# Another order of issue for the steps of a DeltaNet and MLP-mixer kernel

## The chip, the cores and the metric

The kernel runs on one core of a Trainium2 chip, as one program with one launch. The core has a matrix engine (TensorE, PE in the profile, with its weight loads shown apart as PEld), three engines for elementwise work (VectorE, DVE; ScalarE, ACT; GpSimd, POOL) and SyncE (SP), which here issues the DMA transfers. Each of them works through its own instructions strictly in the order in which the program issued them, and waits at an instruction until what it needs is there.

The metric is the time on the device in microseconds, as the median of several runs.

## The reference

Four batches of 768 tokens go through eight heads of a DeltaNet attention (head size 48), and its output, 384 wide, through an MLP mixer that mixes first over the tokens and then over the channels. All values are float32.

```python
k_n = k / (np.linalg.norm(k, axis=-1, keepdims=True) + 1e-06)   # q, k, v: (4, 8, 768, 48)
state = np.zeros((B, H, D, D)); y = np.zeros_like(q)
for t in range(S):
    kt, vt, bt = k_n[:, :, t], v[:, :, t], beta[:, :, t, None]
    y[:, :, t] = np.einsum('bhd,bhde->bhe', q[:, :, t], state)
    v_old = np.einsum('bhde,bhd->bhe', state, kt)
    state = state + bt[:, :, :, None] * np.einsum('bhd,bhe->bhde', kt, vt - v_old)

x = y.transpose(0, 2, 1, 3).reshape(B, S, H * D)                # (4, 768, 384)
xt = x.transpose(0, 2, 1)
h = np.maximum(xt @ w_tok1, 0.0) @ w_tok2                       # 768 -> 256 -> 768
u = x + h.transpose(0, 2, 1)
out = u + np.maximum(u @ w_ch1, 0.0) @ w_ch2                    # 384 -> 1536 -> 384
```

## The kernel before

The attention is computed in chunks of 64 tokens: inside a chunk a triangular matrix made from the keys is inverted, and from chunk to chunk a state of 48 x 48 for each head is carried on. The kernel divides the work into 24 *units* of 128 tokens of one batch (all eight heads, two chunks). Units 0 to 5 are batch 0, 6 to 11 batch 1, and 12 to 23 batches 2 and 3 in turn. The inversion takes units in rounds: round 0 is units 0 to 3, round 1 units 4 and 5, round 2 units 6 to 9, and so on to round 6. The recurrence is a chain for each batch, 12 chunks long, in which each link needs the state that the one before left.

Everything is written as *jobs*. A job is a Python generator that issues a few instructions and then yields, so that each `next` of it is one *step*. A step puts its instructions at the end of the queues of the engines that carry them. The text `order` (from line 1775) lists the steps of the whole kernel, 2,610 of them; `p0*5` stands for five steps of job `p0` in a row. The loop behind the text issues them in that order, and nothing else sets the order of the instructions on an engine:

```python
    for word in order.split():
        name, _, n = word.partition("*")
        for _ in range(int(n or 1)):
            next(jobs[name])
```

So a step that stands early in the text may hold up, on an in-order engine, a step behind it that has nothing to do with it, if its own input is late. The jobs, with the lines that appear in the profile:

- `k0` to `k23` load a unit's keys and queries (DMAs issued by SP, lines 391, 420, 444, into `kst` and `pads`); for the first four units ACT copies the keys (line 435). `v0` to `v23` load the values in four pieces on SP, and POOL scales them by beta (lines 457 to 484).
- `b` loads beta for all batches (line 252), turns it with small products (48 in the profile) into `p_b` (line 257), and ACT copies the result to `beta_st` (line 261). The scaling of keys and values needs it.
- `p0` to `p23` prepare a unit: ACT squares the keys (line 539), DVE sums them (542), ACT takes the square root (547, 548), DVE the reciprocal and its product with beta, `cs` (551, 552), PE transposes keys and queries (562, 582), ACT copies them out of PSUM (566, 587), and POOL makes the mask `mb` from `cs` (574).
- `c0` to `c23` and `d0` to `d11` are a unit's products of keys with keys and queries, `p_g` (PE, line 511, 32 for a unit of batches 0 and 1), with DVE's mask multiplication after them (517).
- `t0` to `t23` cut these into the small pieces that the inversion works on (lines 674 to 686; from unit 6 on through DRAM, `n_dram`). `i0` to `i6` are the rounds of inversion, nearly all DVE (lines 731 to 760). `f0` to `f23`, `h0` to `h11` and `j0` to `j23` put the inverted pieces together again (697 to 711; 777 to 795, among them ACT's copies on line 795; 813 to 892).
- `r0` to `r11` are the recurrences of batch 0, chunk by chunk, `r12` to `r23` those of batch 1 (lines 920 to 972; ACT copies the chunk's new values out of `p_w` on line 950), and `r24` to `r35` those of batches 2 and 3 together (1009 to 1091).
- `m0` and `m1` are the mixer for batches 0 and 1 (products on lines 1593, 1608, 1668 and 1689). Batches 2 and 3 go through `T2`, `T3`, `W`, `S`, `s`, `l` and the groups `A`, `F`, `B` (from line 1098 to 1583), in which products are saved by sums and differences of blocks.
- `w0` to `w33` bring in the mixer's weights, one block of 128 rows each. The weights come as 64-bit words; SP loads a block into one of three buffers `d64` that are used in turn (line 280), two ACT steps (286, 287), one on DVE (289) and one on POOL (293) make rounded float32 of it, and POOL's step frees the buffer. `q0` to `q5` put part of the last weights aside in DRAM.
- `x`, `z` and `Y` compute nothing that is used. `x` is one product of zeros, 128 columns wide (line 235), `z` the same with four times the columns, and `Y` a group of four small products of zeros (line 245; the profile shows each float32 product as two, so eight). They go to a PSUM buffer `p_warm` that nothing else uses in this part of the kernel, and wait for no data.

## Time and profile before

| | us |
|---|---|
| Three runs: lowest, median, highest | 620.05, 625.72, 627.02 |
| The profiled execution, first to last instruction (span) | 619.7 |

The span leaves out only what lies around the first and the last instruction; the profiled execution stands beside the fastest of the three runs.

Engine shares of the whole span hide a good deal here, since it has stages of different kinds: an opening in which the first units are loaded and prepared, the inversion of the first four units, the chain of recurrences with the preparation of later units, from the end of batch 0's on with its mixer beside the rest, and last the mixer of batches 2 and 3. The page's view by slices (40 of 15.5 us each, busy share in tenths) shows where each engine works:

```profile
DVE  5987875986889855697566996866888898685874
ACT  8758796448521344223551215415352331414200
POOL 2348264225311122003020120010000000000000
DMA  9667567667653254454445443135102012020001
```

ACT and DMA are busy at the front, DVE throughout, and POOL nearly only in the first third. The costliest groups of the page are those of the mixer: its columns are line, engine, operation, tiles and forms, count, then busy time and mean ns of one, then idle time just before it and what ended most of that.

```profile
L1668 PE MATMUL p_c<-u_t,wc 128*128 128x256 f32 x432 | 101.6, 386 | 0.5 <-issue 0.5
L1689 PE MATMUL p_o<-wc,r 128*128 128x192 f32 x360 | 64.6, 331 | 0.7 <-DVE xb L1628 0.7
```

The clock that was granted to PE, the row `PEclk`, stands in tenths of full speed for each slice.

### The profile page before, as it was taken

The numbers are of one execution on the slowest core, as the hardware profiler recorded it, in microseconds if no ns is written. First come the engines' busy times: TensorE is split into PE (matmuls) and PEld (weight loads), VectorE is DVE, ScalarE is ACT, GpSimd is POOL, SyncE is SP. The second block draws the span as 40 slices with busy tenths as digits, with TensorE's granted clock in tenths as the row PEclk, the third lists the DMA queues.
The fourth block names the chain that finished last, engine by engine and source line by source line (L and its number), as shares of the span: only waits on it lengthen the run. The fifth ranks groups of instructions, "written<-read, shape, count | busy, mean of one in ns | idle before, by whom it ended". The sixth has DMA issues, their size and how long they took to land.

```text
span 619.7 us, 20909 instructions
## 1 busy us (share of the span) xinstructions
PE 590.3 (95%) x8733; PEld 515.9 (83%) x8733; DVE 469.1 (76%) x1160; ACT 256.9 (41%) x682; POOL 109.9 (18%) x150
## 2 busy tenths in 40 slices
...
DVE  5987875986889855697566996866888898685874
ACT  8758796448521344223551215415352331414200
POOL 2348264225311122003020120010000000000000
PEclk9878797999999999999999999999999999999999
DMA  9667567667653254454445443135102012020001
GB/s 219 136 135 169 138 142 185 129 155 179 126 114 72 67 116 83 95 113 99 92 87 126 83 95 83 32 66 140 32 2 39 1 21 47 12 52 13 14 26 51
DMA packets 154605, 55.52 MB, mean 90 GB/s; under 512 B 129648, under 2 KB 148976, under 8 KB 154512
## 3 DMA queue, kind: packets, MB, share of 16 engines
...
q14 instruction: 25, 0.20, 0.1%
...
## 4 chain that ended last, share of the span: by engine, by line
PE 74%; DVE 9%; DMA 4%; ACT 4%; issue 2%; SPq 1%; POOL 1%; DVEq 0%; POOLq 0%; ACTq 0%
PE p_c L1668 13%; PE p_r L1498 13%; PE p_o L1689 10%; PE p_a L1570 7%; PE p_b L1570 6%; PE p_g L511 3%; DMA d<-in_moe_w_ch_dram 3%; PE p_h L1608 3%; DVE sub L739 2%; PE p L1593 2%; DVE x L744 2%; PE p_k L920 2%; PE p L1223 1%; PE p_h L1238 1%; PE p_y L1034 1%
## 5 line engine op out<-in xcount | busy, mean ns | idle before, releaser
L1668 PE MATMUL p_c<-u_t,wc 128*128 128x256 f32 x432 | 101.6, 386 | 0.5 <-issue 0.5
L1668 PEld LDWEIGHTS p_c<-u_t,wc 128*128 128x128 f32 x432 | 79.6, 190 | 11.9 <-issue 1.1
L1689 PE MATMUL p_o<-wc,r 128*128 128x192 f32 x360 | 64.6, 331 | 0.7 <-DVE xb L1628 0.7
L739 DVE TENSOR_TENSOR sub<-x 128x84 f32<-128x84 f32 (+24 forms) x178 | 58.4, 328 | 7.4 <-DMA x<-n_dram 2.8
L744 DVE TENSOR_TENSOR x<-x,sub 128x84 f32<-128x84 f32 (+24 forms) x178 | 58.2, 327 | 6.1
L1689 PEld LDWEIGHTS p_o<-wc,r 128*128 128x128 f32 x360 | 58.4, 190 | 2.3 <-DVE xb L1628 1.3
L1677 ACT ACTIVATE r<-p_c 128x512 f32<-128x512 f32 x36 | 21.4, 596 | 51.2 <-PE p_c L1668 46.1
L511 PE MATMUL p_g<-kq 48*64 48x128 f32 (+1 forms) x704 | 34.9, 283 | 4.0 <-ACT kq L587 3.3
L517 DVE TENSOR_TENSOR gm<-p_g,mb 128x512 f32<-128x512 f32 x44 | 28.9, 683 | 8.1 <-PE p_g L511 7.5
L484 POOL TENSOR_TENSOR v_st<-v_st,nrm 128x384 f32<-128x384 f32 x12 | 10.3, 856 | 131.9 <-DMA v_st<-in_v_dram 104.4
L574 POOL TENSOR_TENSOR mb<-mask_c,cs 128x512 f32<-128x512 f32 x20 | 21.2, 1062 | 67.8 <-DVE cs L552 36.9
L511 PEld LDWEIGHTS p_g<-kq 48*64 48x64 f32 (+1 forms) x704 | 26.5, 137 | 7.6 <-ACT kq L587 4.3
L293 POOL TENSOR_TENSOR wc<-w_f,d 128x384 uint32<-128x384 uint32 x24 | 24.6, 1029 | 42.8 <-ACT d L287 14.1
L1511 DVE TENSOR_TENSOR kq<-kq,p_r 128x384 f32<-128x384 f32 x40 | 21.0, 551 | 10.7 <-PE p_r L1498 8.8
L1498 PE MATMUL p_r<-t_d,wc 128*128 128x192 f32 x160 | 28.8, 326 | 0.0
L1511 DVE TENSOR_TENSOR gm<-gm,p_r 128x384 f32<-128x384 f32 x40 | 21.1, 551 | 8.1 <-PE p_r L1498 5.8
L400 DVE STREAM_TRANSPOSE kq<-pads 128x512 f32<-128x512 f32 x24 | 25.5, 1108 | 2.0 <-PE p_w L1038 1.6
L1498 PEld LDWEIGHTS p_r<-t_d,wc 128*128 128x128 f32 x160 | 26.5, 190 | 0.0
L1689 PE MATMUL p_o<-wc,s 128*128 128x192 f32 x144 | 25.7, 330 | 0.6 <-DVE xb L1628 0.6
L1498 PE MATMUL p_r<-pads,wc 128*128 128x192 f32 x128 | 25.4, 326 | 0.0
L1628 DVE TENSOR_TENSOR xb<-xb,p_o 128x192 f32<-128x192 f32 x42 | 14.6, 348 | 13.0 <-PE p_o L1689 12.6
L1689 PEld LDWEIGHTS p_o<-wc,s 128*128 128x128 f32 x144 | 23.3, 190 | 1.2 <-DVE xb L1628 0.9
...
## 6 DMA issues: line engine op xcount, KB each, us to landing
...
```

The costliest lines, as they stand in the source:

```text
L293: nc.gpsimd.tensor_tensor(out=dst.bitcast(U32), in0=f, in1=lo, op=ALU.add)
L400: nc.vector.transpose(kq_of[p // 2][:, i, :, p % 2].rearrange("f p (s g) -> f p g s", g=G), rows_of[i].rearrange("s p (g d) -> s p g d", g ...
L511: nc.tensor.matmul(p_g[PAR[i ^ cc ^ swap(u)], p], kqt[f, p, cc, 0], kqt[f, p, cc])
L517: nc.vector.tensor_tensor(out=blocks(gm_of(u))[:, :, cc, D:GW].rearrange("s p (two n) -> s p two n", two=2), in0=p_g, in1=made[u][:, :, cc ...
L739: nc.vector.tensor_tensor(out=tmp, in0=y[:, :, 0:s, s : s + 1].to_broadcast([n, k, s, w]), in1=y[:, :, s : s + 1, s + 1 : m].to_broadcast( ...
L744: nc.vector.tensor_tensor(out=y[:, :, 0:s, s + 1 : m], in0=y[:, :, 0:s, s + 1 : m], in1=tmp, op=ALU.add,)
L1498: nc.tensor.matmul(p[:, i], pieces[q // width][:, at : at + 128], f[f"u{n}"], start=first and i == 0, stop=True, skip_group_check=True,)
L1511: nc.vector.tensor_tensor(out=o, in0=o, in1=p, op=op_of(sign))
L1570: nc.tensor.matmul(p, a[:, i], w[:, i // 2, i % 2], start=first and i == 0, stop=True, skip_group_check=True,)
L1668: nc.tensor.matmul(p_c[:, k], piece_of(wc1, cb, f * 128)[:, f * 128 : (f + 1) * 128], u_t[:, cb], start=(cb == 0), stop=(cb == NCB - 1),)
L1677: nc.scalar.activation(r2[:, m], p_c, ACTF.Relu)
L1689: nc.tensor.matmul(p, a[:, m], wc2[:, m, j], start=(start and i == 0), stop=(i == NM - 1), skip_group_check=True,)
```

## The change

Only the text `order` is replaced. Every job is run through as before, each job's own steps keep their order, and the counts of `x` (8), `z` (10) and `Y` (6) stay the same; so the same 2,610 steps are issued, and each engine carries the same instructions in another order. The first nine words, from `w10` to the second `k1*3`, are the same.

In the opening, `b` now stands ahead of `k0`, where its last steps stood behind `k0` and the first of `p0`. The loads `k2`, `k4`, `k5`, `v0`, `v1` and `w6` move forward, `w18`, `w13`, `w17`, `k7` and `k8` back. In the recurrences the preparation of units 8 to 11 and the loads of weights (`w22`, `w24`, `w26`, `w4`, `w19`, `w7`, `w32`) are placed anew. The number of steps issued between a weight's load and its step on ACT, before and after:

| | w22 | w4 | w19 | w32 | w7 | w13 | w18 | w12 | w17 |
|---|---|---|---|---|---|---|---|---|---|
| before | 1 | 1 | 40 | 3 | 2 | 32 | 68 | 83 | 1 |
| after | 8 | 13 | 40 | 1 | 3 | 1 | 2 | 1 | 1 |

The place of a step in the text, counted from the first step: `r8` begins at 613 before and 605 after, `r9` at 643 and 649, `r11` at 749 in both, `m0` at 676 and 684. The six `Y` stood at 106, 231, 234, 748, 864 and 885 and stand at 37, 225, 227, 639, 640 and 641; the `z` stood at 5, 8, 16, 20, 23, 47, 213, 218, 219 and 256 and stand at 5, 8, 16, 22, 23, 158, 159, 200, 201 and 206; the later `x` moved from 123, 161, 166 and 212 to 132, 133, 152 and 157.

The diff, cut to the part from the first step to a little past `r11`; the rest of the text is permuted in the same manner:

```diff
@@ -1773,76 +1773,90 @@
     jobs["y"] = jobs["Y"] = warm_tiles()
     order = """
-    w10 x*4 z w10*2 z w1*4 k1*3 z k1*3 z b p1 z p1 k0*6 p0*2 b*2 p1 w2 p0*5 p1*2
-    w10 p0*2 z w3 w2 c0*3 p0 w3*2 d0*2 w3 c0 p1 c0 d0*3 k2*3 v1 p1*2 w18 k2*2 p1*2
-    c1*2 d1 k2 p2*2 c1 t0 d1 c1*2 d1*3 t0 p2*8 c2*2 w2 d2 c2*3 Y d2 w2 k3*6 p3
-    d2*2 p3 d2 t1*3 x p3*7 c3 k4*5 k7 w13 w18*2 d3*2 v1*2 v0*2 c3*3 v0 c3 d3*3 t0
-    p4*2 t2*3 x t3*2 p4*2 x t3 i0*2 w13 p4*2 w18 w17*2 i0 k4 i0*9 p4 i0*2 p4*2 c4
-    k8 c4*3 w13*2 w6*2 k5*2 v0 k6 k5*2 i0*2 d4*2 k5 x z d4*3 c4 z*2 p5*2 k5 t4 p5
-    h0 h1 h0 w8*2 h1 Y i0 f0 Y p4 f1 h2*2 p5*3 f0*2 w6 h0*5 k6*5 p6 z f2*2 k8*3 p5
-    w6 p5 p3 p5 j0*3 f1*2 h1*5 j0*2 w8*2 w17 f2 h2*3 v0 t4*2 w17 r0*5 p6 h2*2 c5*2
-    v1 w11*2 j1 p5 k7*2 c5 k7 c5 r0 c5 r0*2 w14*2 v1 w11*2 k7*2 p7 d5*5 r1*5 w14*2
-    p6*2 t5 j1 t5*2 r1*2 j1 j2 p7 h3*2 r1*3 p6*3 i1*2 r2*5 k8*2 f3*2 w9 k9*3 j1*2
-    v2*2 i1*3 j2*2 r2*2 f3 i1*2 p6*3 w16 v2 w16*3 r2*2 h3 r2 i1 d6 r3*5 i1*2 w9*3
-    v2 d6 h3 v2 w0 h3*2 r3 h3 d6*2 w0 d6 j3 c6*5 r3*4 w0 j2 w0 p8*2 j2 r4 p8 r4*4
-    k9*3 j3*2 r4*2 i1*2 w24 i1*2 p7*7 r4 c7 r4 r5*5 k10 p9 k10 p9 c7 r4 c7*3 i1
-    w5*2 p7 r5*2 w24*3 r5*3 j3*2 i1 r6*4 w26 v3*5 p9 k11 r6 d7*5 w26*3 p8*3 t6*2
-    r6*2 w5*2 p8*4 v4*2 t6 i1 r6*3 h5*2 h4*2 k10*2 f4*3 c8*2 k10 p10 w28*2 c8*2 r7
-    c8 r7*3 d8*4 p9 d8 w28 h4*5 p9 t6 r7*2 j4 w28 p9*3 r7*2 p9 w7 d9 w7 v4*2 f5*2
-    w27*2 w7*2 d9*4 c9*2 f5 c9*3 t7*2 t8 r7*2 t7*2 j4*2 v4 p10*2 h5 r8*3 w29 t8*3
-    w29 w27*2 r8*2 w29*2 q3 w29 j4*2 r8 w22*4 t9*3 r8*3 p9 r9 p10 r9*3 t9 v5 h5*3
-    j5 i2 r9 w4*2 r8 h5 i2*5 w4 i2 w19*2 k10 w32 p10*2 w32 v7 k12 m0*2 k11 k12 q0
-    v5*3 p10*2 r9*2 j5*2 k11*3 i2*2 r9 w4 i2 j5 i2*3 p10 v5 r9*2 d10*3 r10 v7*2 j5
-    i2*2 r10*4 w12 i2 k12 i2*2 m0 w32 k11 k12 w32 r10*2 m0 p11 k12*4 w19 p11 r10
-    c10 r10 c10 r10 w33 d10*2 q2 Y r11*4 v7 r11*3 w19 c10 q1 w30 c10 r11 k12*2
-    i2*3 r11 v6*4 i2*5 m0*3 i2*5 q5 i2 m0 p11*4 c10 p11 m0 p11*2 m0*2 k12*2 w12
...
+    w10 x*4 z w10*2 z w1*4 k1*3 z k1*3 p1*2 z*2 b*3 k0*6 k2 p0*2 v1 Y p1 v1 p1*3
+    k2 p0*3 w2 p0*5 c0*2 w10 w2*2 d0*2 k2 c0*2 d0*2 c0 d0 w3 k2 k3 w3 k2 k3 k2 w3
+    p1*3 d1 p1 w6 w3 v0 d1 w2 p2 d1 c1 d1 c1 p2 d1 t0 k3 c1 k3 c1*2 k4 p2*3 v0
+    p2*5 t0 c2*2 k3 k5 k3 d2*3 c2 p3*2 w6*2 c2 d2*2 c2 p3*6 x*2 p3 d3*2 c3 d3*2
+    k4*5 t0 d3 t1 p4 c3*3 x c3 w18 w6 w18 x z*2 p4 t2 t1 t2 t1 t2 t3*3 w8 i0 k5
+    p4 k5*2 w8 k5 i0 p5 i0*2 p4 i0 k5 p4 k6 p4 w8 w0 i0 k7 i0 p4 k6*3 p4 v1*2 w0
+    z*2 w18 p4 i0 w8 z c4*2 i0*2 c4 i0*2 d4 c4 w13*2 w18 i0*2 c4 d4 i0*2 Y d4 Y
+    v1 d4*2 k6*2 i0 h1 w0 v0*2 w17*2 h0 h1 t4 f1*2 f0 f1 f0*2 h0 w13*2 p3 w17 h2
+    f2 h2 p5 w11 p5 w0 h0 f2 p4 h0*2 f2 h0*2 p5*2 k7 p5*2 k8 p5 j0 t4 v0 j0 p5 j0
+    h1 w17 h1*3 j1 h1 j0*2 d5*5 c5 p6*2 r0 w11 r0*2 c5*3 k7 w27 c5 r0 k7 r0 p6 h2
+    k7 h2 r0*2 h2*3 r0 h3 k7 t4 t5 p6 r1*4 k8*5 w11*2 r1 h3 j1 j2 t5*2 f3*3 r1*2
+    j1 i1 p6*3 w16 p7 r1 p6 p5 r1*2 v2 p6 w5 p6 j1 r2 j1 w27 r2*2 k9 r2 j2 r2 w27
+    i1*2 d6 r2*2 w27 p7 w16*2 j2 d6*3 r2 p7 w16 r2 r3*2 d6 r3 r2 r3 k10 r3 v2*2
+    p7 p8 i1 c6*5 h3*3 i1 k9 h3 r3*2 j2 h3 j2 k10*2 j3 p7 i1*2 w5*2 v2 w14 r3
+    p7*2 r3 k9 i1 j3 r4*2 p8 r3 w28 v2 w14 r4*2 k9 r4 v3 k9 p7 r4 i1*4 p7 c7*4
+    w14 j3 r4 w5 k11 c7 r4 p7 i1 k9 r4 d7*3 w9 i1 w28*2 i1 r5*2 w9 w14 t6 w9 v3
+    r4 p9 r5 w28 r5*2 d7*2 j3*2 r5*2 w22 i1 w9 p8*4 r5 w22 h4 k11 h4 r5*2 r6 k11
+    p8*3 i1 v3*2 r6*3 v3 r6 h5 v4 h5 r6*2 c8*2 p9 w22 p9 c8 w22 w24 c8*2 f4 d8
+    r6*2 d8*3 p8 r6 r7 d8 r7*4 v4 w24 v4 t7 v4*2 p9*2 w24 w26 t7 f4 p9 t7*2 r7*2
+    p9*3 k10*2 w26 p10 t6*2 t8 r7 t8*2 r7 t8 c9*4 f4 c9 k11 t6 w19 d9*5 w24 r8*3
+    f5 h4 f5 r8 f5 t9*4 h4 w26 h4*3 r8 h5 k11 h5*3 j4*2 j5 h5 j4 q0 p10 j4 r7 j4
+    w19 Y*3 r8*3 w19 r8 p11*2 r9*4 j5 p10*2 r9 w26 k10 i2 r8 i2*2 j5 w4 q3 r9
+    i2*4 p10 r9*3 i2 j5 w4*2 r9 j5 p10*2 w19 m0 i2*5 p10 r10*3 p10 c10 d10 k12
+    w32*2 d10 v5*2 w7 w32 i2 w7 d10*2 i2*2 r10 v5 m0 v5 m0 v5 r10 k11 p9 c10 r10
+    i2*2 d10 w4 c10 k12 p11 q1 i2 k12*2 p11 r10 v7 i2 r10 w29 w32 w12*2 r10*2 q2
+    v7 p10 p11 c10 r11*3 i2 k12*2 r11 p11 w7 m0 i2 r11*2 i2 c10 k12 i2 w29*2 q5
+    k12*4 w7 i2*2 p11 w12 w29 i2*4 k12 v7 w30 i2 v6 r11 p11 r11 v6*2 m0 v6 r11
...
     """
     for word in order.split():
         name, _, n = word.partition("*")
```

104 lines of the change are left out of this document (57 added, 47 removed).

## The prediction

> **What bounds the kernel now.** I read the page first (span, engines, granted clock), then the busy times by stage, then the opening and two later stretches engine by engine, and the chain of waits last.
>
> ```profile
> span 619.7 us, 20909 instructions
> PE 590.3 (95%) x8733; PEld 515.9 (83%) x8733; DVE 469.1 (76%) x1160; ACT 256.9 (41%) x682; POOL 109.9 (18%) x150
> PEclk9878797999999999999999999999999999999999
> ```
>
> PE is busy 95% of the span, but the granted clock dips, and only in the first seven slices of 15.5 us. So the next view is the busy time of each engine by stage; its columns are PE, PEld, DVE, ACT, POOL, then granted clock, DMA share and GB/s. I cut at the start of the first inversion (26.7), its end (43.7), recurrence 0 (52.0), recurrence 8 (96.7) and recurrence 11 (121.1).
>
> ```profile
> 0.00:26.70 26.70, 20.14 (x246) 14.70 (x246) 18.14 (x54) 22.22 (x58) 7.96 (x22) 1.00 0.75 171
> 26.70:43.70 17.00, 11.66 (x129) 7.79 (x130) 15.22 (x39) 6.87 (x17) 6.40 (x6) 0.70 0.79 171
> 43.70:52.00 8.30, 7.04 (x205) 5.68 (x201) 7.23 (x13) 7.90 (x23) 6.44 (x8) 1.00 0.45 90
> 52.00:96.70 44.70, 41.22 (x1228) 36.47 (x1227) 35.39 (x89) 38.02 (x103) 25.25 (x32) 0.89 0.68 155
> 96.70:121.10 24.40, 19.95 (x402) 14.41 (x397) 18.18 (x53) 12.66 (x35) 8.06 (x11) 0.79 0.68 162
> 121.10:619.70 498.60, 490.25 (x6549) 436.84 (x6545) 374.98 (x915) 169.21 (x450) 55.81 (x73) 1.00 0.33 73
> ```
>
> The reader is to see two regimes. After 121.1 us PE works 490.25 of 498.60 us at full clock: another order of the same products can gain at most the 8.35 us left idle there. Before it PE idles 21 us and loses clock, and the limit changes: ACT in the opening (22.22 of 26.70), DVE during the first inversion (15.22 of 17.00), ACT from there to recurrence 8 (7.90 of 8.30, then 38.02 of 44.70), and nothing saturated from 96.7 to 121.1, where waits set the pace. So the change is decided before recurrence 11.
>
> **The change part by part.** Every job keeps its number of steps, x, z and Y too: no work is added or removed, only each engine's queue is reordered. Each part is priced as the shift of a milestone. ACT carries most of them, so its rows come first, in order of time.
>
> ```profile
> 6.97 0.52 ACT L539 ACTIVATE ksq<-kst 128x384 f32<-128x384 f32 x1
> 7.74 1.43 ACT L435 COPY kst<-pads 64x192 f32<-64x192 f32 x4 [0.25 <-DMA pads<-in_k_dram]
> 9.21 0.52 ACT L539 ACTIVATE ksq<-kst 128x384 f32<-128x384 f32 x1
> 9.64 0.48 ACT L261 COPY beta_st<-p_b 128x192 f32<-128x192 f32 x1
> 11.27 0.59 ACT L587 COPY wc<-p_t 128x512 f32<-128x512 f32 x1
> ...
> 38.55 0.72 ACT L754 ACTIVATE r<-r,odd 128x512 f32<-128x512 f32 x1 [4.89 <-DVE r L753]
> 52.77 0.32 ACT L950 COPY rw_t<-p_w 128x192 f32<-128x192 f32 x1
> ...
> 90.56 1.08 ACT L795 COPY gm<-p_x 16x128 f32<-16x128 f32 x4
> 97.13 0.30 ACT L548 ACTIVATE ksum<-nrm,eps 128x8 f32<-128x8 f32 x1
> 97.34 0.54 ACT L286 ACTIVATE d<-d 128x384 f32<-128x384 f32 x1
> 97.78 0.54 ACT L287 ACTIVATE d<-d 128x384 uint32<-128x384 uint32 x1
> 101.02 0.55 ACT L286 ACTIVATE d<-d 128x384 f32<-128x384 f32 x1 [1.93 <-DMA d<-in_moe_w_ch_dram]
> 106.94 0.44 ACT L286 ACTIVATE d<-d 128x256 f32<-128x256 f32 x1 [3.88 <-DMA d<-in_moe_w_tok_dram]
> 111.67 0.56 ACT L286 ACTIVATE d<-d 128x384 f32<-128x384 f32 x1 [1.42 <-DMA d<-in_moe_w_ch_dram]
> ```
>
> ```profile
> 7.83 1.57 PE L257 MATMUL p_b<-pick,b_rows 32*64 32x16 f32 x48
> 11.91 1.37 PE L511 MATMUL p_g<-wc 64*64 64x128 f32 x32 [0.18 <-ACT wc L587]
> 30.31 1.09 PE L582 MATMUL p_t<-ident,pads 128*128 128x128 f32 x4 [5.38 <-DMA pads<-in_q_dram]
> ```
>
> *The opening, up to the first inversion.* Job b (beta's load, 48 products into p_b, ACT's copy of them) now stands ahead of k0's copies. The same nine x and z products stand ahead of p_b in both orders, so p_b still ends near 9.4. Before, ACT did k0's copies and square (1.43 + 0.52) while p_b ran; now it waits from 7.49 (6.97 + 0.52) to 9.4 and does them afterwards. That is 2.0 us, on the engine that bounds the opening. Ahead of the inversion's first step ACT also gains w6's pair (1.1, as at 97.34 and 97.78) and loses p4's square root and square (0.5): +0.6. Sum: the inversion starts 2.6 us later, at 29.3. Bounds: +1.4 (w6's pair falls into a pause of ACT, and 0.6 of the wait is made up) to +3.8 (1.2 more, were POOL's w6, now ahead of t1 to t3, to hold these up).
>
> *SP in the opening.* k2, k4, k5, v0, v1 and w6 are issued earlier, w18, w13, w17, k7 and k8 later. Unit 4's queries came late before, behind k7's load, w13, w17 and pieces of v1 and v0; PE idled 5.38 us for them (the row of 30.31). Now they precede k7, and that idle goes. I price it at zero: DVE, inverting without a pause, covers it; if that cover were gone it would be worth 5.4 us. The load of w13 now stands two steps ahead of the POOL step that frees its buffer (three buffers d64, in turn), and w11 likewise behind w0. SP waits there, with k6's last loads, two pieces of v0 and w17 queued behind, which ACT and POOL need only after the inversion, past ACT's wait of 4.89 us. Taken 0; bounds 0 and +3.9 (the longest wait on a weight above, 3.88).
>
> *Inside the first inversion.* DVE does its steps back to back.
>
> ```profile
> 26.23 0.20 DVE L551 RECIPROCAL ksum<-ksum 128x8 f32<-128x8 f32 x1
> 26.47 0.17 DVE L552 TENSOR_TENSOR cs<-ksum,beta_st 128x8 f32<-128x8 f32 x1
> 35.89 0.35 DVE L289 TENSOR_SCALAR w_f<-d 128x384 uint32<-128x384 uint32 x1
> 40.01 1.27 DVE L517 TENSOR_TENSOR gm<-p_g,mb 128x512 f32<-128x512 f32 x2
> ```
>
> The new order puts p4's pair (0.37), w8 and w18 (0.35 each) and half of unit 4's masking (0.64) between them and takes w13 (0.35) out: +1.4. ACT's row of 38.55 comes 2.6 + 1.4 = 4.0 us later; bounds of this part +0.6 (part of it in short pauses of DVE) and +1.4. ACT's own added work (1.4) lies in its 4.89 us wait. From there to recurrence 0's copy (52.77) ACT's work is the same within 0.1: that copy comes 4.1 us later, at 56.9.
>
> *Recurrence 0 to 8.* ACT bounds. Thirteen instructions leave the place ahead of recurrence 8 (h4's four, w7's two, f5's, r7's, j4's and p10's pairs): the first is the row of 90.56, the last that of 97.13, together 4.8 us. w22's pair comes (1.1). The pairs of w11 and w0 (2.0), less two of h2's copies (0.5), had been done ahead of recurrence 0. Work between the two: -3.7 - 1.5 = -5.2. ACT is busy 0.85 of that stage, so I credit -4.4; bounds 0 and -5.2. Recurrence 8 starts 0.3 us earlier, at 96.4.
>
> *Recurrence 8 to 11.* The 3.7 come back, with 0.5 more: +4.2 of ACT work. ACT is busy only 12.66 of 24.40 us, so I charge that share, +2.2 (bounds 0 and 4.2). Against it ACT waited 1.93, 3.88 and 1.42 us, 7.2 in all, on the loads of w22, w4 and w32, whose ACT steps stood 1, 1 and 3 steps behind their issue. Now they stand 8, 13 and 1 behind (w19 40, w7 3). One wait stays, w32's; at the longest, 3.88, that leaves -3.3. Bounds 0 and -7.2.
>
> *Zeros and clock.* Three groups Y move ahead of recurrence 8, from beside recurrence 11 and after.
>
> ```profile
> 55.20:58.60 3.40, 2.73 (x102) 2.42 (x100) 3.32 (x7) 2.70 (x8) 2.63 (x4) 1.00 1.00 240
> 58.60:68.80 10.20, 10.20 (x243) 9.20 (x240) 7.92 (x22) 7.31 (x20) 3.80 (x5) 0.50 0.58 129
> 96.10:99.50 3.40, 2.55 (x102) 2.20 (x97) 2.13 (x5) 2.84 (x8) 2.70 (x3) 1.00 0.74 171
> 99.50:109.80 10.30, 7.48 (x77) 5.12 (x70) 5.97 (x21) 4.67 (x14) 3.90 (x6) 0.50 0.77 209
> ```
>
> ```profile
> 120.30 0.44 PE p_warm L245 x8
> ```
>
> Each of these half-clock stretches follows 3.4 us in which PE had a hundred small products and short pauses. The three Y fall into the second such window. Its half clock costs at most half of 7.48, 3.7 us. I take half, -1.8 (bounds 0 and -3.7), because 58.6 lost its clock with PE busy 2.73, not far below what Y would make of 2.55. Two of the moved groups ran after 121.1, where PE bounds, 0.44 each: -0.9. The x and z groups move within stretches where PE waits: 0.
>
> The Trainium skill, "TensorE: Matmul & The Clock Gate", Part 1, says that an idle window of about 3.4 us drops PE to half clock. The trace agrees where PE idled 5.38 us (the inversion's stage has a mean clock of 0.70), but 58.6 lost its clock with PE busy. By the rule alone, Y would hold the clock at 99.5 (-3.7 in place of -1.8, a sum of -6.0), and the idle in the new opening would cost it there; the first rival prices that from rows.
>
> *After recurrence 11.* Same products, 8.35 us idle: 0, and half of that idle, 4 us, either way as bounds.
>
> *Sum* against the profiled execution: 4.1 - 4.4 + 2.2 - 3.3 - 1.8 - 0.9 = -4.1 us, 615.6 instead of 619.7. That execution equals the fastest of the three runs (620.05); their median is 625.72, and no row says why. Carried to the median: 621.6, 0.7% less.
>
> **The rivals.** *The late opening stays (slower).* If the chain of recurrences, each needing the state before, sets the pace and not ACT's load, the opening's delay arrives whole. And it grows if PE loses its clock in the opening: with its transposes done near 11, it waits for the first p_g until about 14.5 (11.91, plus 2.0, plus one copy as at 11.27, now ahead).
>
> ```profile
> 32.07 2.04 PE L511 MATMUL p_g<-kq 64*64 64x128 f32 x24 [0.68 <-ACT kq L587]
> ```
>
> That row is p_g at half clock: 2.72 us for a unit's 32 products, against 1.37 at full clock (11.91). Three units: +4.1. Price 4.1 + 4.1 - 0.9 = +7.3: 633.0. It decides once recurrence 0's copy comes after 60. For it: PE waits 3.5 us in the opening. Against it: ACT busy at 85% up to recurrence 8.
>
> *All waits on weights go and the clock holds (faster).* -7.2 and -3.7 in place of -3.3 and -1.8: 4.1 - 4.4 + 2.2 - 7.2 - 3.7 - 0.9 = -9.9, 615.8. For it: most loads stand further ahead. Against: w32 and w7 stand close behind theirs.
>
> *The shifts before recurrence 11 cancel.* The change then does little of what the queues suggest, and only the two Y count: 624.8. For it: the work of each of PE, DVE and ACT queued ahead of recurrence 11 differs by 0.5 us at most.
>
> **How the numbers follow.** Forecast 0.34, faster rival 0.30, slower rival 0.22, cancelling 0.14. Within 1% (619.5 to 632.0, about what a measurement of this kernel can tell from no change) lie the forecast and the cancelling: 0.48; faster 0.30, slower 0.22. The range, 613 to 634, reaches to the slower rival and 3 us past the faster one, for the bounds after 121.1; a tenth is left out at each end. The forecast's own range is 617 to 626.
>
> **What would show it.** Right: p_b's copy on ACT near 9.5 with k0's copies behind it, the first p_g near 14.5, the first inversion near 29, recurrence 0's copy near 57, recurrence 8 near 96, no ACT wait of over 1 us on w22 or w4, clock 1.0 at 100 us. Wrong: the first p_g near 12, recurrence 0 before 54 or after 60, recurrence 11 more than 6 us off 117, or PE's idle after it changed by over 5 us.

## The result, and the profile after

The change made the kernel slower: 658.14 us (median of 4 runs, 657.29 to 658.94) against 624.89 us, a ratio of 1.055 with a 95% interval of 1.0501 to 1.0599. The forecast was 621.6 us (613 to 634). The profiled execution spans 656.8 us, 37.1 us more than before's 619.7; the medians lie 33.3 us apart. Medians and ratios below leave out executions that took over 1.5% longer than the fastest of the same kernel (one each of h_r0, f17 and, with 1481 us, z_inv, and two of a_r12), and the traces of h_r0 and a_r12 are of such ones, so times read from these two are rough.

The page of the kernel after, first its span, busy times and the clock by slices, then the chain that ended last; behind it the same chain of the kernel before.

```profile
span 656.8 us, 20903 instructions
...
PE 605.0 (92%) x8733; PEld 526.8 (80%) x8733; DVE 472.3 (72%) x1160; ACT 257.4 (39%) x682; POOL 110.6 (17%) x150
...
PEclk9966989779999999999969999999999999999999
...
PE 52%; DVE 23%; DMA 9%; SPq 7%; issue 4%; ACT 4%; POOL 0%; DVEq 0%; ACTq 0%
PE p_r L1498 12%; PE p_o L1689 7%; DVE x L744 6%; PE p_a L1570 6%; DVE sub L739 6%; PE p_b L1570 6%; PE p_c L1668 4%; DMA gm<-w_dram 3%; PE p_g L511 2%; SPq L711 2%; SPq L444 2%; DMA x<-n_dram 2%; PE p L1223 1%; DVE gm L517 1%; PE p_h L1238 1%
```

```profile
PE 74%; DVE 9%; DMA 4%; ACT 4%; issue 2%; SPq 1%; POOL 1%; DVEq 0%; POOLq 0%; ACTq 0%
PE p_c L1668 13%; PE p_r L1498 13%; PE p_o L1689 10%; PE p_a L1570 7%; PE p_b L1570 6%; PE p_g L511 3%; DMA d<-in_moe_w_ch_dram 3%; PE p_h L1608 3%; DVE sub L739 2%; PE p L1593 2%; DVE x L744 2%; PE p_k L920 2%; PE p L1223 1%; PE p_h L1238 1%; PE p_y L1034 1%
```

The instructions are the same and as many on every engine, yet the chain passes over from PE to DVE, DMA and SP: PE, the bound before, now waits for others. Lines 739 and 744, the steps of the inversion, hold 12% of the chain in place of 4%. PE's clock dips in one slice in the middle too: the mean granted clock of the span is 0.947 in place of 0.975, which comes to some 70 us at half clock in place of 31 (twice the share that is missing, times the span).

Next the busy time by stage, cut at the same events as in the prediction (start and end of the first inversion, starts of recurrences 0, 8 and 11).

```profile
0.00:29.30 29.30, 22.81 (x254) 16.74 (x255) 18.32 (x52) 23.54 (x61) 9.92 (x23) 0.94 0.83 193
29.30:47.60 18.30, 6.98 (x99) 4.99 (x98) 16.61 (x41) 4.90 (x11) 6.52 (x7) 0.74 0.43 101
47.60:59.80 12.20, 11.23 (x214) 10.48 (x216) 6.27 (x14) 9.63 (x28) 8.53 (x11) 0.50 0.51 122
59.80:102.20 42.40, 36.50 (x1152) 32.45 (x1144) 33.74 (x84) 34.31 (x93) 21.27 (x27) 0.93 0.61 134
102.20:136.10 33.90, 25.34 (x522) 18.93 (x515) 23.40 (x62) 15.93 (x45) 8.23 (x10) 0.76 0.60 152
136.10:656.80 520.70, 502.14 (x6527) 443.25 (x6523) 373.91 (x911) 169.09 (x448) 56.13 (x73) 0.98 0.31 69
```

Against the stages before (26.70, 17.00, 8.30, 44.70, 24.40, 498.60 us) this is +2.6, +1.3, +3.9, -2.3, +9.5 and +22.1 us. So more than half of the loss lies behind recurrence 11, where the forecast had put nothing. That long stage, in three parts of the kernel before and then of the kernel after, from r12 to the round of inversion i4, from there to i5, and on to the first step of group A, shows how:

```profile
143.42:250.00 106.58, 104.89 (x1869) 92.36 (x1865) 75.66 (x185) 44.29 (x128) 24.59 (x30) 1.00 0.47 103
250.00:333.40 83.40, 82.86 (x1448) 68.66 (x1447) 57.93 (x146) 28.86 (x85) 13.05 (x18) 1.00 0.47 100
333.40:442.00 108.60, 106.01 (x1918) 89.41 (x1918) 85.76 (x227) 35.90 (x105) 11.51 (x17) 1.00 0.37 85
```

```profile
158.93:273.40 114.47, 109.68 (x1808) 94.73 (x1805) 77.03 (x190) 43.61 (x123) 24.04 (x31) 1.00 0.46 101
273.40:362.60 89.20, 85.67 (x1500) 71.15 (x1499) 57.53 (x145) 30.42 (x92) 12.08 (x16) 0.94 0.45 97
362.60:478.60 116.00, 109.73 (x1920) 91.61 (x1919) 89.23 (x231) 35.48 (x103) 11.60 (x17) 0.97 0.32 75
```

PE's idle time (length less busy time) goes from 1.7, 0.5 and 2.6 us to 4.8, 3.5 and 6.3, and the clock leaves 1.00 twice. Over the whole last stage PE's idle time grew from 8.35 to 18.56 us. The clock was at half for some 21 us there (the last part of a stretch that ends at 140.4, then 331.6 to 341.8, 423.8 to 427.2 and 457.9 to 461.3) and before for none, which costs half of that at most. The two together, an estimate from these rows, are at most 21 of the 22.1 us. What DVE waited for names the other end: rows of the groups of instructions, first before, then after, with the idle time ahead of them and what ended it.

```profile
L739 DVE TENSOR_TENSOR sub<-x 128x84 f32<-128x84 f32 (+24 forms) x178 | 58.4, 328 | 7.4 <-DMA x<-n_dram 2.8
...
L744 DVE TENSOR_TENSOR x<-x,sub 128x84 f32<-128x84 f32 (+24 forms) x178 | 58.2, 327 | 6.1
...
L813 DVE STREAM_TRANSPOSE t<-gm 128x256 f32<-128x256 f32 x22 | 9.6, 438 | 8.2 <-PE p_z L846 5.5 <-PE p_z L851 1.4 <-DMA gm<-w_dram 0.8
```

```profile
L744 DVE TENSOR_TENSOR x<-x,sub 128x84 f32<-128x84 f32 (+24 forms) x178 | 68.1, 383 | 6.1
...
L739 DVE TENSOR_TENSOR sub<-x 128x84 f32<-128x84 f32 (+24 forms) x178 | 60.3, 339 | 14.9 <-DMA x<-n_dram 10.8
...
L813 DVE STREAM_TRANSPOSE t<-gm 128x256 f32<-128x256 f32 x22 | 9.7, 443 | 23.2 <-DMA gm<-w_dram 18.4 <-PE p_z L851 2.9 <-ACT gm L795 1.2
```

The first steps of the rounds of inversion (`i`, line 739) and of the joins (`j`, line 813) wait for loads that come back from DRAM: 3.6 us in all before, 29.2 after. And line 744, whose instructions are the same, takes 383 ns each, against 327 before.

### The profile page after: what moved, and what is told of

It reads as the page before. It is cut to its first block, busy times and chain, and to the rows that moved or that the text cites. A ratio compares the mean times of both kernels' runs of the same rounds, so it can differ in the third digit from the quotient of the medians.

```text
span 656.8 us, 20903 instructions
## 1 busy us (share of the span) xinstructions
PE 605.0 (92%) x8733; PEld 526.8 (80%) x8733; DVE 472.3 (72%) x1160; ACT 257.4 (39%) x682; POOL 110.6 (17%) x150
## 4 chain that ended last, share of the span: by engine, by line
PE 52%; DVE 23%; DMA 9%; SPq 7%; issue 4%; ACT 4%; POOL 0%; DVEq 0%; ACTq 0%
PE p_r L1498 12%; PE p_o L1689 7%; DVE x L744 6%; PE p_a L1570 6%; DVE sub L739 6%; PE p_b L1570 6%; PE p_c L1668 4%; DMA gm<-w_dram 3%; PE p_g L511 2%; SPq L711 2%; SPq L444 2%; DMA x<-n_dram 2%; PE p L1223 1%; DVE gm L517 1%; PE p_h L1238 1%
## 5 line engine op out<-in xcount | busy, mean ns | idle before, releaser
L1668 PE MATMUL p_c<-u_t,wc 128*128 128x256 f32 x432 | 103.5, 393 | 0.4 <-issue 0.4
L1668 PEld LDWEIGHTS p_c<-u_t,wc 128*128 128x128 f32 x432 | 81.6, 194 | 12.7 <-issue 1.0
L744 DVE TENSOR_TENSOR x<-x,sub 128x84 f32<-128x84 f32 (+24 forms) x178 | 68.1, 383 | 6.1
L739 DVE TENSOR_TENSOR sub<-x 128x84 f32<-128x84 f32 (+24 forms) x178 | 60.3, 339 | 14.9 <-DMA x<-n_dram 10.8
L1689 PE MATMUL p_o<-wc,r 128*128 128x192 f32 x360 | 66.2, 333 | 1.3 <-DVE xb L1628 1.3
L511 PE MATMUL p_g<-kq 48*64 48x128 f32 (+1 forms) x704 | 36.7, 288 | 3.5 <-ACT kq L587 1.2
L813 DVE STREAM_TRANSPOSE t<-gm 128x256 f32<-128x256 f32 x22 | 9.7, 443 | 23.2 <-DMA gm<-w_dram 18.4
```

The source lines that it names most:

```text
L511: nc.tensor.matmul(p_g[PAR[i ^ cc ^ swap(u)], p], kqt[f, p, cc, 0], kqt[f, p, cc])
L739: nc.vector.tensor_tensor(out=tmp, in0=y[:, :, 0:s, s : s + 1].to_broadcast([n, k, s, w]), in1=y[:, :, s : s + 1, s + 1 : m].to_broadcast( ...
L744: nc.vector.tensor_tensor(out=y[:, :, 0:s, s + 1 : m], in0=y[:, :, 0:s, s + 1 : m], in1=tmp, op=ALU.add,)
L1668: nc.tensor.matmul(p_c[:, k], piece_of(wc1, cb, f * 128)[:, f * 128 : (f + 1) * 128], u_t[:, cb], start=(cb == 0), stop=(cb == NCB - 1),)
L1689: nc.tensor.matmul(p, a[:, m], wc2[:, m, j], start=(start and i == 0), stop=(i == NM - 1), skip_group_check=True,)
```

## The experiments: in which stretch the time is lost

Since a job's steps keep their order, two orders can be joined at any step: one order up to it, then what is left in the other. At such a junction the two orders differ by 14 to 23 steps that one has issued by then and the other not, which has a price of its own. Six such kernels were run; the table gives their ratio to the kernel before.

```diff
 # h_r0, h_r12, h_m1, h_i5: X = the first step of r0, r12, m1, i5
-order = after
+order = before[: index of X] + [steps of after that are not yet issued]
 # a_r0, a_r12: X = the first step of r0, r12
-order = after
+order = after[: index of X] + [steps of before that are not yet issued]
```

> The order before up to the first step of r0, then all that is left in the order of the changed kernel. In the traces r0's first copy on ACT comes at 62.1 us in the changed kernel and at 52.8 before. Theory (what is lost ahead of r0 is carried to the end): 658.1 - 9.3 = 649, between 647 and 651. Rival (the later waits, on transfers and on DVE, swallow the opening's delay): 655 to 659.

> The order before up to the first step of r12, then what is left in the order of the changed kernel. r12 starts at 158.9 us in the changed kernel and at 143.4 before. Theory (carried to the end): 658.1 - 15.5 = 643, between 640 and 645. Rival (the loss between r0 and r12 is only the opening's, once more visible): like the run with the order before up to r0, 649.

> The order before up to the first step of m1, then what is left in the order of the changed kernel. m1 starts at 293.4 us in the changed kernel and at 271.8 before. Theory (the rest of the new order loses another 15 us by itself, in its own waits): 658.1 - 21.6 = 636.5, between 634 and 640. Rival (the late losses come from the early ones, as transfers that were late by then): 625 to 629.

> The order before up to the first step of i5, then what is left in the changed order. Of the 16.8 us that the run with the order before up to m1 lost in its profile, 10.3 were lost by the time of i5. Theory (losses are local): 624 + 6 to 7 = 630 to 631. Rival (all of the late loss stems from the stretch of r26 to r28 and its clock): 624 to 626.

> The order of the changed kernel up to the first step of r0, then all that is left in the order before. Theory (the opening's 9 us are carried on): before + 7 to 9 us, 631 to 633. Rival (the run with the order before up to r0 saved only 1.5 us, so what comes later swallows the opening's delay): before + 0 to 3 us.

> The order of the changed kernel up to the first step of r12, then all that is left in the order before. Theory (losses are local to the stretch in which the new order stands, and add up): the run with the two orders the other way round took 14 us less than the changed kernel, so before + 12 to 15 us, 636 to 639. Rival (the rest of the order before makes part of it up, as the waits there have slack): before + 5 to 8 us.

| order before, then after from | ratio (95%) | median us | order after, then before from | ratio (95%) | median us |
|---|---|---|---|---|---|
| the start | 1.055 (1.050 to 1.060) | 658.1 | | | |
| r0 | 1.051 (1.044 to 1.058) | 654.2 | r0 | 1.014 (1.009 to 1.019) | 633.0 |
| r12 | 1.032 (1.025 to 1.040) | 645.5 | r12 | 1.024 (1.020 to 1.029) | 639.2 |
| m1 | 1.019 (1.012 to 1.025) | 635.5 | | | |
| i5 | 1.009 (1.006 to 1.013) | 629.6 | | | |

Read downwards, the new order loses something in each stretch: between r0 and r12 1.9% by the left column and 1.0% by the right one, from r12 to m1 1.3%, from m1 to i5 and from i5 to the end 0.9% each. The opening, up to r0, costs 1.4% when the rest is as before. The kernel with the old opening saved only 0.4% by the ratios, with intervals that overlap, and its median lies between the theory's range and the rival's. Its junction spoils it as a test of the opening: by r0 the new order has done the grams of unit 5, weight block w0 and more, the old one h2 and loads of k8; behind the old opening the new order puts that work ahead of r0, and in its trace recurrence 0's copy came at 60.55 (+7.8 us, though the opening is the old one) and r8's first product at +13.2, against +9.4 and +5.5 in the changed kernel. The step from r0 to r12 in the left column holds that price too. The theory of local losses came nearer in the other five: h_m1 and a_r0 lie within its ranges, h_r12, h_i5 and a_r12 up to 0.5 us outside. And in a_r0 and a_r12 the delay that was there at r12 (12.8 and 25.9 us in the traces) was still there at the end (11.5 and 25.9): behind r12 the order before made hardly any of it up.

## The experiments: the opening and the first inversion

*PE's empty queue and its clock.* In the kernel after, unit 4's queries come early, so PE does the transposes, the grams and the zeros without a pause and is done at 34.2 us. Then:

```profile
34.20:45.30 11.10, 0.02 (x2) 0.00 (x0) 9.69 (x29) 2.32 (x5) 5.55 (x7) 0.67 0.41 102
45.30:62.00 16.70, 15.67 (x285) 14.95 (x286) 9.77 (x18) 10.82 (x30) 8.53 (x11) 0.50 0.45 102
```

```profile
45.36 1.92 PE L777 MATMUL p_z<-r,wc 64*64 64x32 f32 x32 [11.14 <-DVE r L755]
62.12 0.32 ACT L950 COPY rw_t<-p_w 128x192 f32<-128x192 f32 x1 [1.62 <-PE p_w L944]
```

PE stands still for 11.1 us, waits for the inversion's last step (line 755), and then works 15.67 of 16.70 us at half clock until recurrence 0's copy at 62.12: here PE is the pace. From the first product of the joins to that copy it takes 16.8 us, and 11.9 before (40.82 to 52.77). Two kernels tested it, one on either side.

```diff
 # z_inv, from the kernel after
-    v1 d4*2 k6*2 i0 h1 w0 v0*2 w17*2 h0 h1 t4 f1*2 f0 f1 f0*2 h0 w13*2 p3 w17 h2
+    v1 d4*2 k6*2 i0 z*12 h1 w0 v0*2 w17*2 h0 h1 t4 f1*2 f0 f1 f0*2 h0 w13*2 p3 w17 h2
 # no_z, from the kernel before
-    k8 c4*3 w13*2 w6*2 k5*2 v0 k6 k5*2 i0*2 d4*2 k5 x z d4*3 c4 z*2 p5*2 k5 t4 p5
+    k8 c4*3 w13*2 w6*2 k5*2 v0 k6 k5*2 i0*2 d4*2 k5 d4*3 c4 p5*2 k5 t4 p5
```

> The changed kernel with twelve products of zeros (z) ahead of h1's first step, where PE stands idle from 34.2 to 45.4 us; 10 us of work that nobody needs. Theory (idle PE loses its clock, and the half clock from 38.1 to 62.0 us makes the steps from the inversion to r0 longer): the clock stays 1.0 from 38 to 62, r0's first copy comes 3 to 5 us earlier than 62.1, time 653 to 655. Rival (DVE, ACT and the transfers set the pace there): clock 1.0, but r0 within 1 us of 62.1 and 657 to 659.

> The kernel before without four of its products of zeros (one x and three z that PE works through at 35 to 39 us, while the first inversion runs on DVE): less work, and nothing else changed. Theory (PE that stands idle during the inversion loses its clock, and the joins behind it are too small to win it back): half clock from about 38 to 41 us until 60 or later, r0's first copy on ACT at 56 to 58 us in place of 52.8, time 2 to 5 us more than before. Rival (the clock does not matter there, DVE and ACT set the pace): r0 within 1 us of 52.8, time within 1 us of before.

z_inv: 662.4 us, ratio 1.059 (1.050 to 1.069), no gain. The first row is the stretch with the zeros, the second the joins up to r0.

```profile
34.20:46.60 12.40, 11.47 (x50) 5.24 (x47) 10.96 (x31) 2.44 (x5) 6.53 (x7) 1.00 0.37 91
46.60:62.40 15.80, 13.69 (x274) 12.83 (x276) 9.54 (x17) 10.81 (x30) 8.49 (x11) 0.57 0.45 104
```

The zeros held the clock as long as they ran, and two microseconds into the joins it fell all the same: 13.69 us of busy PE at a mean of 0.57. Recurrence 0's copy came at 62.83; its inversion had begun 1.2 us later than in the kernel after. So what was to be tested, joins at full clock, did not come about, and the empty queue is not the whole cause: with PE busy up to the joins, the clock fell within them. The order before also has two Y and a z among its joins (at 42.68 and 46.06 us in its trace) which the new one issues ahead of them; no run put those back.

no_z shows what such products are worth in the kernel before. Without one x and three z, which nobody uses, it became slower, 626.7 us, ratio 1.006 (1.003 to 1.009):

```profile
42.00:47.20 5.20, 5.19 (x82) 5.20 (x84) 4.95 (x7) 4.00 (x11) 1.80 (x2) 0.50 0.54 100
```

PE idles 5.71 us before the joins' first product at 42.01, and they then run at 0.50 until 47.6 us (1.00 in that place before). The half clock that begins at the wait for unit 4's queries ends at 38.1 us with the zeros (27.9 to 38.1) and at 47.6 without (30.5 to 47.6). Recurrence 0's copy is 3.6 us later, of which 1.2 were there already when the inversion began. It isn't one execution alone: the mean clock of the span is 0.970 over the twelve of no_z and 0.976 over the 23 of the kernel before beside them. Those zeros were worth 0.6%, by keeping PE busy in a gap; the change keeps their number and moves them out of it.

More zeros, in turn, do not help the kernel before:

```diff
 # more_z, from the kernel before: z*6 ahead of p4's eighth step, z*2 ahead of r8's eighth
-    p4*2 t2*3 x t3*2 p4*2 x t3 i0*2 w13 p4*2 w18 w17*2 i0 k4 i0*9 p4 i0*2 p4*2 c4
+    p4*2 t2*3 x t3*2 p4*2 x t3 i0*2 w13 p4*2 w18 w17*2 i0 k4 i0*9 p4 i0*2 z*6 p4*2 c4
```

> The kernel before with six more products of zeros ahead of p4's second transposes, where PE idles 5.4 us before the half clock of 27.9 to 38.1 us, and two ahead of r8's state product, where it idles 2.0 us at the start of the half clock of 99.5 to 109.8 us. Theory (idle PE loses its clock there): no half clock from 28 to 38, recurrence 9 earlier, time 1 to 3 us less than before. Rival (DVE paces the inversion, and a small window of few products loses the clock with or without the idle): within 1 us of before, or slower by the 1.7 us of the two products.

626.5 us, ratio 1.004 (1.002 to 1.007): the half clock moved from 27.9 to 40.4 us, into the joins, and recurrence 0 came 3.3 us later, of which 1.0 was there already at the inversion's start. Over twelve executions the mean clock was higher than in the kernel before, 0.980 against 0.977, and the time longer, so the amount of half clock alone does not decide (the eight added steps of zeros are work too). The rival held; the gap before p4's transposes is no place for them.

*POOL's work beside the inversion.* In the kernel after four POOL instructions of about a microsecond that read SBUF fall into the inversion. The timeline of its second half, DVE's steps of line 744 and then POOL's, start and duration:

```profile
36.24 0.27 DVE L744 TENSOR_TENSOR x<-x,sub 128x108 f32<-128x108 f32 x1
37.01 1.00 DVE L744 TENSOR_TENSOR x<-x,sub 128x112 f32<-128x112 f32 x1
38.35 0.78 DVE L744 TENSOR_TENSOR x<-x,sub 128x112 f32<-128x112 f32 x1
39.47 0.27 DVE L744 TENSOR_TENSOR x<-x,sub 128x108 f32<-128x108 f32 x1
```

```profile
36.87 1.00 POOL L293 TENSOR_TENSOR wc<-w_f,d 128x384 uint32<-128x384 uint32 x1 [1.08 <-DVE w_f L289]
...
38.14 0.86 POOL L460 TENSOR_TENSOR v_st<-v_st,nrm 128x384 f32<-128x384 f32 x1
38.94 2.01 POOL L619 MEMSET z<- 128x2304 f32 x1
```

Each slow DVE step starts behind a POOL instruction and ends with it (37.01 + 1.00 = 38.01 beside 36.87 + 1.00 = 37.87, and 38.35 + 0.78 = 39.13 beside 38.14 + 0.86 = 39.00). The one at 36.24, with POOL still, takes 0.27, as does the one at 39.47, beside the fill with a constant (line 619). To measure it by itself, the kernel before got POOL work in that place:

```diff
 # pool_in, from the kernel before; g_t is a new tile of 128x120
+    def extra_pool():
+        while True:
+            nc.gpsimd.tensor_tensor(out=g_t, in0=g_t, in1=g_t, op=ALU.add)
+            yield
...
-    p4*2 t2*3 x t3*2 p4*2 x t3 i0*2 w13 p4*2 w18 w17*2 i0 k4 i0*9 p4 i0*2 p4*2 c4
+    p4*2 t2*3 x t3*2 p4*2 x t3 i0*2 y*12 w13 p4*2 w18 w17*2 i0 k4 i0*9 p4 i0*2 p4*2 c4
```

> The kernel before with twelve small additions on POOL (128x120, on a tile that nothing else uses) issued at the start of the first inversion, some 4 to 5 us of POOL work that DVE doesn't need. Theory (a DVE instruction of two operands stands until a POOL instruction that has started ends): several of the inversion's instructions on lines 739 and 744, 0.19 to 0.28 us each before, take up to twice that, and the inversion is 1.5 to 3.5 us longer than its 13.4 us. Rival (they do not disturb each other): 13.4 us as before.

```profile
33.09 0.45 DVE L739 TENSOR_TENSOR sub<-x 128x100 f32<-128x100 f32 x1
33.57 0.95 DVE L744 TENSOR_TENSOR x<-x,sub 128x100 f32<-128x100 f32 x1
34.55 0.99 DVE L739 TENSOR_TENSOR sub<-x 128x108 f32<-128x108 f32 x1
35.59 0.27 DVE L744 TENSOR_TENSOR x<-x,sub 128x108 f32<-128x108 f32 x1
```

Beside POOL's additions (0.39 us each) the steps take 0.45 in place of 0.26, beside POOL's longer ones 0.95 and 0.99, and 0.27 as soon as POOL is still. The inversion, from the end of its first step to its last scaling, took 14.2 us against 11.4, and the kernel 627.5 us, ratio 1.006 (1.003 to 1.009). The effect is shown. The Trainium skill, "SBUF — State Buffer", section "SBUF: two separate sides", says that a DVE instruction with two inputs in SBUF and a GpSimd instruction that reads SBUF exclude each other for their whole length; the traces agree, the fill included, which reads nothing.

This also answers for line 744's 383 ns. In the kernel after 51 instructions of lines 739 and 744 run beside a POOL instruction that isn't a fill, and 23 before; beyond the shortest with the same operands they take 16.4 us and 4.4. The other 305 and 333 take 0.9 and 1.2 us more in all, the eight beside fills included. Of the 16.4 us 2.9 lie in the first inversion (0.9 before), and 6.2 between 100 and 160 us (1.0 before), where the chain that ended last runs through these lines from the load of i2 on. No run took POOL's work out of these places, so what they cost the kernel after is not measured; the new order has 12 us more of them on DVE.

Two runs moved weights, and POOL's steps, in the kernel after:

```diff
 # w_late, from the kernel after: 20 steps moved, in the order of issue
-w0, w13, w17, w11 (4 steps each) at steps 188 to 337; w27 at 307 to 381
+w13.0 w17.0 w0.0 behind r0; w13.1-3 w11.0 and w17.1-3 within r1; w0.1-3 ahead of r2;
+w11.1-3 w27.0 ahead of r3; w27.1-3 within r3
 # w_pool, from w_late
-w8.3 at step 205, w18.3 at 218, v1.4 at 228
+w8.3 w18.3 v1.4 ahead of h1
```

> The run before with three steps of POOL (w8's and w18's addition, v1's scaling) also moved out of the first inversion to its end. Theory (a DVE instruction of the inversion that meets a busy POOL stands until POOL's instruction ends, at 0.26 us of its own and 0.8 to 1.1 as seen): the products on line 744 that took 1.05, 1.00 and 0.78 us at 34.9, 37.0 and 38.4 us take 0.27 each, and the inversion's last steps come 1.8 to 2.3 us earlier than in the run before. Rival (they were slow for another reason, a transfer that writes beside them): as slow as before.

> The changed kernel with the weight blocks w13, w17, w0 and w11 brought in behind r0 (spread over r0 to r3) in place of during and right after the first inversion; w27 goes behind r3. Theory (the waits of SP on the weights' buffers, 3.7 and 11.9 us in the changed kernel, and the weights' steps on DVE and POOL between the inversion and r0 make r0 late): both waits of SP are gone, r0's first copy on ACT comes at 57 to 59 us in place of 62.1, and the time falls by 3 to 5 us to 653 to 655. Rival (r0 waits for PE at half clock): r0 within 1 us of 62.1, time within 2 us of the changed kernel's.

In w_pool (one execution, 665.7 us) nothing moved in the inversion, so it doesn't test the theory. POOL's queue held nothing else in between, so POOL took the three steps as early as before: a step that is only moved in the text past other engines' steps is not delayed. w_late removed SP's waits and brought r0's copy to 61.3 in place of 62.1, not to 57 to 59: the theory fell, and PE at half clock, the rival, stands. It cost time instead, 666.4 us, ratio 1.066 (1.061 to 1.071). The weights' pairs on ACT now fell between r0 and r3, and r4's first product of `p_w` came 13.5 us later than before, against 7.7 in the kernel after. That ACT is the bound in that stage, as the prediction took it, does not follow: from r0's first such product to r4's ACT is busy 20.85 of 29.34 us, against 19.17 of 22.69 in the kernel after, and the clock has a mean of 0.73 against 0.95.

*Beta's copy.*

```diff
 # b_late, from the kernel after
-    w10 x*4 z w10*2 z w1*4 k1*3 z k1*3 p1*2 z*2 b*3 k0*6 k2 p0*2 v1 Y p1 v1 p1*3
+    w10 x*4 z w10*2 z w1*4 k1*3 z k1*3 p1*2 z*2 b*2 k0*6 k2 p0*2 b v1 Y p1 v1 p1*3
```

> The changed kernel with the copy of beta on ACT (b's last step) behind k0's copies and p0's first steps, as it stood before. Theory (the opening's 2.0 us of the prediction are ACT's wait for p_b): the first inversion starts 2.0 us earlier, at 29.3 in place of 31.3 (end of its first step), and at most that much of the time is saved, 656 to 658. Rival (the opening is late because of the loads' new order): the inversion starts within 0.5 us of 31.3.

655.0 us, ratio 1.049 (1.046 to 1.053), an interval that overlaps that of the kernel after. The first product of the grams came 1.4 us earlier (12.64 in place of 14.07), so ACT's wait is real, but the inversion's first step ended where it did (31.5 and 31.3), as the rival has it: half clock lay on 6.8 us of that opening and on 3.4 in the kernel after.

## The experiments: DVE's waits for loads

The longest of DVE's new waits stands at j17, for a load of f17 that SP issues behind k20 and v16:

```profile
329.03 0.45 DVE L813 STREAM_TRANSPOSE t<-gm 128x256 f32<-128x256 f32 x1 [7.02 <-DMA gm<-w_dram]
```

Behind the wait DVE has the state of r26 (line 1066), and PE waits 1.27 us for that at 331.38; the clock is at half from 331.6 to 341.8. Five kernels tried to take such waits away or to make one.

```diff
 # f17, from the kernel after (h_m1_f17: the same move in h_m1)
-    k20*4 r26*2 j15 j14 r25 k20*3 v15 v16*3 f17 m1*2 s f17 m1 k20 j15*2 m1*2 j16
+    f17*2 k20*4 r26*2 j15 j14 r25 k20*3 v15 v16*3 m1*2 s m1 k20 j15*2 m1*2 j16
 # f17_before, from the kernel before
-    p19*2 j14 p19*3 r26*2 f15*4 f14 m1*2 j14 m1 j14 j15*3 s*2 f17*2 m1 f17 m1
-    f16*3 p19 f16 k20*8 j16*3 j17 m1 r26*3 p20 m1*2 p20 r26*2 c19*2 r26 c19 v15
+    p19*2 j14 p19*3 r26*2 f15*4 f14 m1*2 j14 m1 j14 j15*3 s*2 f17 m1*2
+    f16*3 p19 f16 k20*8 j16*3 f17*2 j17 m1 r26*3 p20 m1*2 p20 r26*2 c19*2 r26 c19 v15
 # h_i5_add, from h_i5
-    t20 s t20*3 t21*4 s r26 v17*3 k22 r27 m1*4 v17 i5*4 m1*2 r29*3 k22*3 r29
+    t20 s t20*3 t21*4 s r26 v17*3 k22 r27 m1*4 v17 i5 m1*2 i5*3 r29*3 k22*3 r29
 # undo3, from the kernel after: the edits of b_late and f17, and
-    m1*2 t21 v17 t21 i5*4 m1*2 r29*3 k22*3 r29 i5 k22 i5 k22*2 r29 r28 i5 r28
+    m1*2 t21 v17 t21 i5 m1*2 i5*3 r29*3 k22*3 r29 i5 k22 i5 k22*2 r29 r28 i5 r28
```

(In the first of these expectations "48 lines of text" is a slip; j17 first stands one line further on.)

> The changed kernel with two loads of unit 17's inverted parts (f17, 48 lines of text later used by j17) issued ahead of the loads k20 and v16 and not behind them. In the changed kernel DVE stood 7.0 us at j17 (322.0 to 329.0 us) for that load, with the state's update of r26 behind it, and PE ran dry and lost its clock at 331.6 for 10.2 us. Theory: DVE's wait falls below 1 us, the clock stays 1.0, time 5 to 7 us less, 651 to 653. Rival (DVE waits for the same data behind other steps, or PE had no work left in any case): 656 to 659.

> The run with the order before up to m1 and the changed order after it, with the two loads of f17 ahead of the loads k20. There DVE stood 6.8 us at j17 (302.9 to 309.6 us) and PE ran dry for 1.2 and 1.6 us. Theory (a loss in the late part is local and stays): 3 to 5 us less than the 635.5 of that run, 631 to 632. Rival (given back at the next wait on a load, as in the run with f17 moved in the changed kernel): 634 to 636.

> The kernel before with two loads of unit 17's inverted parts (f17) issued behind the loads k20, directly ahead of j17 that needs them, as late as they are in the changed kernel. Theory (DVE waits at j17 for the load, with the recurrence's state behind it, PE runs dry): j17 some 5 us later than at 299.6 us, and the time 3 to 6 us more than before. Rival (a late load costs its wait there and no time at the end, since PE's queue holds work and later waits shrink): within 1.5 us of before.

> The run with the order before up to i5 and the changed order after it, with one edit: the mixer's two steps m1*2 stand between the load of i5's input and the DVE steps that use it, and not behind them. In that run DVE stood 5.0 us at i5's first step for the load, the mixer's addition (line 1628) behind it kept a PSUM buffer, PE idled 2.5 us for that buffer and lost its clock for 3.4 us. Theory (what stands behind a waiting DVE instruction makes PE run dry): the addition comes before the wait, PE's idle of 2.5 us goes, and of the 629.6 us 2 to 4 are saved, 626 to 628. Rival (PE runs dry at the next buffer, or the loss shows again at i6): 629 to 630.5.

> The changed kernel with three of its places put as before: beta's copy behind k0's copies, f17's loads ahead of k20's, the mixer's two steps ahead of i5's first wait. Theory (each is local and they add up: 3.2 us measured for beta's copy, 0.7 for f17, 2 to 4 for the third): 658 - 6 to 8 = 650 to 652. Rival (given back at other waits, as f17's was): 654 to 657.

| kernel | median us | ratio (95%) | compare |
|---|---|---|---|
| f17 | 656.7 | 1.052 (1.048 to 1.056) | after 1.055 |
| h_m1_f17 | 635.8 | 1.019 (1.015 to 1.023) | h_m1 1.019 |
| f17_before | 625.7 | 1.001 (0.998 to 1.004) | before 1 |
| h_i5_add | 631.9 | 1.010 (1.007 to 1.014) | h_i5 1.009 |
| undo3 | 658.8 | 1.052 (1.048 to 1.057) | after 1.055 |

None of them moved the time by more than its uncertainty. No theory holds: f17, h_m1_f17 and (by its ratio) f17_before lie where the rival has them, h_i5_add and undo3 1.4 and 1.8 us above the rival's range. In f17 the wait itself did go. DVE's wait at j17 fell from 7.02 to 1.63 us, now for PE; the clock stayed at 1.0 there. But at the next such place, i5, DVE waited longer than in the kernel after (5.57 us in place of 1.54), and PE ran dry there. Counted from r12's first product, j17 came 4.7 us earlier than in the kernel after and i5 0.5 us later. The rows of f17 at i5, DVE's and then PE's:

```profile
367.02 0.19 DVE L739 TENSOR_TENSOR sub<-x 128x30 f32<-128x30 f32 x1 [5.57 <-DMA x<-n_dram]
```

```profile
368.82 0.69 PE L1689 MATMUL p_o<-wc,r 128*128 128x192 f32 x1 [3.05 <-DVE xb L1628]
```

In h_i5 it is the same place: PE waits 2.48 us for a PSUM buffer which the addition of the mixer (line 1628), queued on DVE behind the wait, has to free. h_i5_add put that addition ahead of the wait. It was then done at 335.43, and PE stood all the same, for the recurrence's values (line 1018), which stand behind the wait too:

```profile
339.04 0.19 DVE L739 TENSOR_TENSOR sub<-x 128x30 f32<-128x30 f32 x1 [3.26 <-DMA x<-n_dram]
```

```profile
342.12 0.25 PE L1038 MATMUL p_w<-rw_t,gm 64*64 64x48 f32 x1 [1.78 <-DVE rw_t L1018]
```

So it is not one instruction that is in the wrong place. The order before has four steps of the mixer between i5's load and its first use, some 4 us of PE work and its additions; the new one has none, and did them earlier. f17_before shows the reverse: there PE's queue held work, and two loads issued late cost DVE 2.2 us more at j17 (5.24 in place of 3.04) and the kernel nothing.

That such cover is what the late stretches lack is our reading of these traces. Shown is that the loss lies in those stretches (the table of joined orders), that DVE's waits for loads on lines 739 and 813 grew from 3.6 to 29.2 us in the kernel as a whole, and that moving single steps does not bring it back. The length of these waits is not the loss by itself: in the trace of undo3 they are 18.6 us, 10.6 less than in the kernel after, and the span is the same (657.5). No run put the cover back as a whole, and POOL's hold on DVE, which grew too, was not tested in these stretches.

## Why the prediction was wrong, point by point

- *The opening, +2.6 us*: measured +2.6 (inversion at 29.30). Its account was right as far as the first grams: beta's copy at 9.43 with k0's copies behind it, the first `p_g` at 14.07. From there to the inversion it was not: with beta's copy put back, the grams came earlier and the inversion did not (b_late), and the clock, which the forecast left at full, was at half for 3.4 us of this opening. That the sum came out to the tenth is luck in part.
- *SP in the opening, taken as 0 since "DVE, inverting without a pause, covers it"*: the first step that failed. The cover was priced for DVE alone. The 5.38 us for which PE had waited for unit 4's queries had held the grams and the zeros back to just ahead of the joins; with them gone, PE is done at 34.2 us, idles 11.1 us, loses its clock at 38.0 and works at half until 61.9. From the joins' first product to r0's copy it takes 4.8 us more than before. What is shown: in the kernel before the zeros in that gap are worth 0.6% (no_z). What is open: which of the moved steps makes the joins of the kernel after run at half clock, since filling its gap alone did not help (z_inv). SP's wait on the buffer of w11 was 11.8 us, three times its upper bound of 3.9; w_late shows that it was not what r0 waited for.
- *Inside the first inversion, +1.4 us*: the stage grew by 1.3, but the last step that the joins wait for (line 755) came 5.1 us later than before, 2.5 more than the start. The stage's length fits by luck, since less of unit 4's work stood on DVE behind that step. Added DVE work was counted; POOL's instructions, which hold DVE's up for their whole length, were not: 2.9 us of DVE's time in this inversion, 0.9 before. Before's own timeline has one such step, which was not read:

```profile
36.39 1.06 DVE L744 TENSOR_TENSOR x<-x,sub 128x28 f32<-128x28 f32 x1
```

```profile
36.38 1.01 POOL L293 TENSOR_TENSOR wc<-w_f,d 128x384 uint32<-128x384 uint32 x1 [7.59 <-issue]
```
- *Recurrence 0's copy at 56.9*: 62.12, +9.4 in place of +4.1. The slower rival's mark (after 60) was reached. Its mechanism, PE losing its clock in the opening, was right in kind; the loss lay behind the inversion, and its price of +7.3 for the whole kernel was a fifth of what came.
- *Recurrence 0 to 8, -4.4 us*: from +9.4 at r0's copy to +5.5 at r8's first step, -3.9, which looks like the forecast. Between like events it is less: from r0's first product (+7.8) to r8's (+5.5) -2.3, from r0's copy to r8's (+7.9) -1.5. The clock was better in that stage too, 0.93 in place of 0.89. What ACT's lighter load was worth is not shown, and w_late doesn't show it either.
- *Recurrence 8 to 11, +2.2 - 3.3 - 1.8 us*: +9.5. What was forecast for ACT came true and was worth nothing: its waits for w22, w4 and w32, 7.2 us before, were down to 0.9, for w4. The pace was set by the load of i2, as the next row shows: DVE waits 4.27 us for it and starts i2 11.4 us later than before. The new order has one step between that load and its first use, the order before five. On DVE r10 stands behind fifteen steps of that inversion (fourteen before), which take 14.1 us in place of 11.2; POOL's instructions hold them up by 2.3 us of this stage, in place of 1.0. So r10 comes 14.3 us later than before. The prediction took ACT's waits for the bound because they were the ones it had rows for; the inversion's chain, from its load through DVE to the next recurrences, has no term in it.

```profile
116.78 0.19 DVE L739 TENSOR_TENSOR sub<-x 128x30 f32<-128x30 f32 x1 [4.27 <-DMA x<-n_dram]
```

- *Zeros and clock, -1.8 us*: the clock was 1.0 at 100 us, as forecast, and fell later, at 113.1 and 130.2. The windows of 3.4 us ahead of these, in the busy times of the kernel after:

```profile
109.80:113.20 3.40, 2.51 (x111) 2.22 (x106) 1.45 (x5) 2.19 (x8) 0.96 (x1) 0.99 0.90 254
126.80:130.20 3.40, 1.05 (x9) 0.27 (x7) 3.26 (x7) 0.00 (x0) 1.99 (x2) 1.00 0.19 25
```

  The first is of the kind that the prediction had shown, PE busy 2.51 of 3.40 us with small products; in the second PE mostly idled. The half clock was not removed: before r11's first product it was at half for more of the time than before (mean clock 0.76 in place of 0.79 in the stage ahead of it).
- *After recurrence 11, "same products, 8.35 us idle: 0", +-4 us*: the largest error, +22.1. The idle time bounds what a better order can gain. It does not bound what a worse one can lose, and the bound was used both ways. The order behind recurrence 11 was permuted as thoroughly as the opening's, and was not walked through. Of the 22.1 us some 10 are added idle time of PE and at most 11 half clock. That the missing work between loads and their use makes both is likely and not shown. The two Y of this stage, -0.9, were not measured by themselves.

In sum, the span was 41.2 us above the 615.6 of the forecast: 5.3 up to recurrence 0's copy, 0.5 from there to r8, 12.4 from r8 to r11 and 23.0 behind. The two terms that were set to zero, since another engine covered them or since PE was busy, stand in the first and the last of these. In the third a sum was worked out, for an engine that did not set the pace. None of the four outcomes that were given chances went beyond 633: no rival had the late stretches lose.
